# A layered attention and gated-GLU kernel: a new feature layout with the first chunk projected from raw weights, residual additions that are due on VectorE, and divided attention operations

## The chip, the cores and the metric

The kernel runs on one core of a Trainium2 chip. A core has a matrix engine (TensorE, PE in the profile, PEld for its weight loads), a vector engine (VectorE, DVE), an activation engine (ScalarE, ACT), a general engine (GpSimd, POOL) and a sequencer that issues the transfers here (SyncE, SP). Each engine runs its own queue in order, and semaphores order the engines among each other. Matmuls write to PSUM, eight banks of 128 partitions by 2 KB; everything else lies in SBUF. The metric is device microseconds of one launch, the median of several executions.

## The reference

Input and output are 2048 tokens of 576 features in bf16. Four layers run one after the other, two of kind A and two of kind B in turn, each with a residual: `x = x + A(norm(x))`, `x = x + B(norm(x))`, and the same pair again with the same weights.

- norm is a layer norm without parameters (mean, variance, eps 1e-5).
- A is local attention: `qkv = x @ wqkv` gives 32 heads of 18 features. Query s looks at 8 keys, at s, s-2, ..., s-14; keys before token 0 are masked. Softmax over the 8, the weighted sum of the values, then `@ wo`.
- B is a gated bilinear block: `h = (x @ w_gate) * (x @ w_up)`, 4608 wide, then `h @ w_down`.

## The kernel before

The tokens are worked off in chunks: `seq` lists 18 of them as (layer pair, first tile, number of 128-token tiles). The first four chunks of the first layer pair have one tile, the other 14 have two. The tokens go in two groups of eight tiles, and within a group first layer pair 0 and then layer pair 1. For every chunk j the program states the operations of `attention(j, ...)` and then of `glu(j, ...)`.

The order of the instructions is not that of the program. Each operation is given to a planner (`Plan.op`) with its engine, an estimated cost in ns, the keys that it reads and writes, a priority and a rank. `Plan.run` (lines 84 to 166) simulates the engines with these estimates and emits operations one by one; within an engine that order is then fixed. It takes the operation that can start first. Where that one has a rank above 0, an operation of a lower rank on the same engine is taken instead if it becomes ready soon enough (SLACK, GUARD, IDLE and LOOK set how soon). Chunk 0's attention has rank 0, chunk j's attention rank j, all GLU work 60; operations marked `due=True` have rank -1. These are the evacuations of the GLU (L901 on ScalarE, L902 on VectorE) and the small copies of `fence` (L471). Where TensorE would wait early on, `fill` (L1067) emits matmuls on zeros.

Attention of a chunk: `head` norms the tokens (bn_stats L414, aggregate L415, rstd by Ln and Exp on ScalarE L429 and L430, the scaled mean L433, the apply L439) and transposes them, for the first five chunks on TensorE (L452, L454) with a copy by ScalarE (L457), later by a DMA. `project` makes q, k and v (L527), which ScalarE, and for chunk 0 VectorE too, bring to SBUF. Scores: VectorE multiplies q with shifted k for two of the eight positions at a time (L676), adds feature blocks (L680 to L685; not for chunk 0), and TensorE adds over the features with the selector Esel (L691). Softmax: the mask for the first tokens (L710), max, subtract, Exp, sum, reciprocal, multiply (L711 to L722). The weights are spread to the features' partitions: for the first five chunks by matmuls with Bsel (L732), later over DRAM (`a_dram`, one write and four reads). VectorE multiplies them with shifted v (L762) and adds (L776; for chunk 0 matmuls with the identity do that, L766 and L767). Then come the output projection (L816 for one tile, L795 for two) and the residual additions on VectorE (L786), two for each tile, and the second `head` for the GLU.

The projection wants the features by (feature, head) and not by (head, feature). So wqkv is loaded in its own order into the scratch area `scr` (L323, q and k first, v after) and 25 copies (L355, 12 on VectorE and 13 on ScalarE) bring it into `wqkv` in the new order. Chunk 0's projection waits for these copies.

The GLU block works in units of 512 columns: gate and up (L866 and L877 for one tile, L890 for two) into a pair of banks, ScalarE copies the gate (L901), VectorE multiplies (L902), TensorE does the down projection (L918 and L919, or L958 and L959), and VectorE adds its result (L929, L938). Output projection and q, k, v use the same pairs of banks ("unit"). The GLU weights come in six slices of columns, the wd tiles in a ring of seven.

```python
    for j, (l, t0, nst) in enumerate(seq):
...
        pool["k"] = "pa" if j else "boot"
        pl.rank = min(j, 50)
        attention(j, l, t0, nst)
        pl.rank = 60
...
        glu(j, t0, nst, l == n_al - 1)
```

Of the kernel before, what the change touches and what calls it, by code (L numbers as in the profile page):

```python
# [16 lines left out]
class Op:  # L17
    __slots__ = ("eng", "cost", "fn", "deps", "order", "succ", "n", "prio", "idx", "hold", "free",
                 "lat", "margin", "ready", "end", "nbytes", "use", "pair", "need", "rank", "late", "half")
# [3 lines left out]
HOLD = 2  # L23
VP = ["ACT"] * 5
VT = ["ACT"] * 5
SLACK = {"DVE": 500, "ACT": 300, "PE": 0, "POOL": 0, "SP": 0}
IDLE = (2000, 300)
GUARD = {"DVE": 300, "ACT": 300, "PE": 600, "POOL": 0, "SP": 0}
TURN = (148, 98)
LOOK = {"DVE": 1, "ACT": 1, "PE": 1, "POOL": 0, "SP": -9}  # L30


class Plan:
# [13 lines left out]
    def op(self, eng, cost, fn, r=(), w=(), prio=1, after=None, hold=None, free=None, margin=0, nbytes=0, use=None,  # L47
           pair=None, need=None, due=False, late=0, half=False):
        o = Op()
        o.rank, o.late, o.half = -1 if due else self.rank, late, half  # L50
# [3 lines left out]
        d = set()  # L54
# [28 lines left out]

    def run(self, slots):
        clock = {e: 0.0 for e in self.LAT}
# [5 lines left out]
        while cand:  # L91
            best = None
            urgent = {}
            for o in cand:
                t = 0.0
                for p in o.deps:
                    e = p.ready if p.eng != o.eng else p.end
                    if e > t:
                        t = e
                t += o.margin  # L100
                if o.hold is not None:
# [10 lines left out]
                t = max(t, clock[o.eng])  # L112
                key = (t, o.prio, o.idx)
# [5 lines left out]
            if o.rank > 0:  # L119
# [34 lines left out]
            if o.free is not None:  # L154
# [3 lines left out]
                if u["left"] == 0:  # L158
                    free[o.free].append((u["last"], u["slot"]))
            o.fn()  # L160
            done += 1
            for s in o.succ:
                s.n -= 1
                if s.n == 0:
# [5 lines left out]
def kernel(  # L170
# [33 lines left out]
    NXS, NWD, NH, NXB, NB = 4, 7, 6, 3, 3  # L204

# [8 lines left out]
    a_dram = [dram.tile([P, 2 * CH], BF16, name=f"a_dram{i}") for i in range(2)]  # L214
# [12 lines left out]
    Bsel = sb("Bsel", [P, 4, 4, 32])  # L227
# [31 lines left out]
    wrawa = scr[:, 0:KT * 2 * D].rearrange("p (k n) -> p k n", k=KT)  # L259
    wrawb = scr[:, 7168:7168 + KT * D].rearrange("p (k n) -> p k n", k=KT)  # L260
# [41 lines left out]
    def load_x(t0, nst, tmp=False):  # L302
# [3 lines left out]
           nbytes=P * nst * D * 2, prio=0 if t0 < 1 else 1.5 if t0 < 2 else 2.5)  # L306
# [11 lines left out]
    def load_w(c):  # L318
        wr, c0, c1 = ((wrawa, 0, 2 * D), (wrawb, 2 * D, 3 * D))[c == "b"]
        for k in range(KT):  # L320
            for r_, rows in ((0, P),) if k < KF else ((0, TL), (TL, TL)):
                def fn(k=k, r_=r_, rows=rows):
                    i = nc.sync.dma_start(wr[r_:r_ + rows, k, :], A_wqkv[k * P:k * P + rows, c0:c1])  # L323
# [777 lines left out]
```

## Time and profile before

| What | Value |
|---|---|
| median of 3 executions | 1062.14 us (1060.86 to 1063.78) |
| profiled execution, its own time | 1063.46 us |
| its span, first to last instruction | 1061.7 us |
| mean granted TensorE clock | 0.996 |
| busy: TensorE, VectorE, ScalarE | 98%, 74%, 39% |
| first GLU matmul | 33.88 us |
| VectorE busy, 60 to 150 us | 77.8 of 90 us |
| VectorE busy, 200 to 600 us | 341.6 of 400 us |
| VectorE busy, 900 to 1000 us | 47.1 of 100 us |

A row of the timeline has start and length in us, engine, line, operation, output <- input, shape and count, and in brackets the engine's idle time before it and what ended that. A row of the waits has who waited for whom, us in total, times and the longest. PEclk is the clock that TensorE was granted, as a share of the full one. A window's row has its bounds, its length, the busy time of the engines asked for, the clock, the DMA engines' mean busy share and their GB/s.

### The profile page before, as it was taken

Reading aid. Unit: us, or ns where it says so; the run is one execution under the profiler, and the core shown is the slowest. Engines: PE = TensorE matmul, PEld = TensorE weight load, DVE = VectorE, ACT = ScalarE, POOL = GpSimd, SP = SyncE. Lnnn points to the kernel's source line nnn. Section 1 sums busy time; section 2 is a strip of 40 time slices with the busy share of each in tenths; the row PEclk is TensorE's granted clock in tenths of the full one; section 3 lists DMA queues with packets and bytes.
Section 4 is the critical chain, followed back from the end, with each engine's and each line's share of the span. In section 5 each row is a group of like instructions: output and inputs, shape, how many; then the busy total and the mean of one; then the engine's idle time right before and its main releaser. Section 6 shows DMA issues by size and latency. Waiting matters only on the chain.

```text
span 1061.7 us, 39938 instructions
## 1 busy us (share of the span) xinstructions
PE 1044.4 (98%) x17864; PEld 839.5 (79%) x17864; DVE 781.6 (74%) x1421; ACT 411.8 (39%) x1090; POOL 8.9 (1%) x33
## 2 busy tenths in 40 slices
PE   7999999999999999999999999999999999999998
PEld 4888878798888878878878887777877778877775
DVE  7688979786969896989798874666788748833332
ACT  6752254342334534423444324324334252233231
POOL 3000000000000000000000000000000000000000
PEclk9999999999999999999999999999999999999999
DMA  9956563623253444345444443243362333443332
GB/s 263 323 184 197 179 178 102 170 69 121 81 147 86 128 103 109 82 126 138 117 93 106 110 143 94 83 147 87 75 173 82 94 94 115 126 127 102 114 102 68
DMA packets 146827, 133.67 MB, mean 126 GB/s; under 512 B 42272, under 2 KB 146016, under 8 KB 146656
## 3 DMA queue, kind: packets, MB, share of 16 engines
q1 hardware_dynamic: 146656, 131.13, 44.1%
q8 instruction: 139, 2.28, 0.9%
q14 instruction: 32, 0.26, 0.1%
HBM read 118.51 MB, written 4.06 MB: 115 GB/s over the span
## 4 chain that ended last, share of the span: by engine, by line
PE 77%; DVE 14%; DMA 5%; ACT 1%; SPq 1%; issue 1%; DVEq 0%; ACTq 0%
PE pu L890 15%; PE pg L890 13%; PE pu L958 5%; PE acct L890 4%; PE pa L958 4%; PE pa L890 4%; PE pg L527 4%; PE pu L527 3%; PE pg L958 3%; PE acct L958 3%; PE pu L866 3%; PE pg L866 3%; PE pg L918 3%; DVE scr L762 2%; DVE oT L776 2%; DVE h L902 2%
## 5 line engine op out<-in xcount | busy, mean ns | idle before, releaser
L890 PE MATMUL pg<-xnT_B,wg 64*128 64x256 bf16 x3072 | 394.8, 270 | 3.2 <-DVE xf L786 3.2
L890 PE MATMUL pu<-xnT_B,wu 64*128 64x256 bf16 x3072 | 394.3, 270 | 1.6 <-DVE xf L938 1.2
L890 PEld LDWEIGHTS <-wg 64*128 64x128 bf16 x4032 | 367.3, 94 | 28.6 <-issue 3.4
L890 PEld LDWEIGHTS <-wu 64*128 64x128 bf16 x4032 | 366.3, 94 | 24.6 <-issue 3.6
L902 DVE TENSOR_TENSOR h<-pu,g_sb 128x512 bf16<-128x512 f32 x228 | 153.7, 686 | 59.4 <-ACT g_sb L901 56.0
L958 PEld LDWEIGHTS <-h 64*128 64x128 bf16 (+1 forms) x1992 | 120.7, 94 | 96.9 <-DVE h L902 1.6
L901 ACT CAST g_sb<-pg 128x512 bf16<-128x512 f32 x228 | 132.2, 586 | 115.8 <-PE pg L890 80.6
L471 ACT COPY tok<-pu 1x1 f32<-1x1 f32 x270 | 39.7, 147 | 308.8 <-PE pu L890 214.5
L959 PE MATMUL pg<-wd,h 64*128 64x64 bf16 (+1 forms) x828 | 157.4, 190 | 1.4 <-DVE xf L786 1.4
L959 PE MATMUL pu<-wd,h 64*128 64x64 bf16 (+1 forms) x828 | 157.4, 190 | 0.3 <-DVE xf L786 0.2
L958 PE MATMUL pg<-wd,h 64*128 64x512 bf16 x600 | 154.9, 377 | 0.3 <-DVE h L902 0.3
L958 PE MATMUL pu<-wd,h 64*128 64x512 bf16 x600 | 154.9, 377 | 0.0
L890 PE MATMUL acct<-xnT_B,wg 64*128 64x256 bf16 x960 | 130.7, 269 | 0.0
L890 PE MATMUL pa<-xnT_B,wu 64*128 64x256 bf16 x960 | 130.7, 270 | 0.0
L959 PEld LDWEIGHTS <-h 64*128 64x128 bf16 (+1 forms) x1992 | 119.2, 95 | 2.1 <-issue 1.7
L527 PEld LDWEIGHTS <-wqkv 64*128 64x128 bf16 (+1 forms) x2044 | 103.9, 94 | 15.5 <-issue 3.8
L676 DVE TENSOR_TENSOR scr<-qT,kv 128x2560 bf16<-128x2560 bf16 (+1 forms) x68 | 89.9, 1326 | 29.9 <-ACT kv L611 29.7
L958 PE MATMUL acct<-wd,h 64*128 64x512 bf16 (+1 forms) x396 | 103.6, 382 | 0.4 <-DVE h L902 0.4
L958 PE MATMUL pa<-wd,h 64*128 64x512 bf16 (+1 forms) x396 | 104.0, 382 | 0.0
L890 PE MATMUL pu<-xnT_B,wgu_t 64*128 64x256 bf16 x384 | 103.5, 270 | 0.0
L890 PE MATMUL pg<-xnT_B,wgu_t 64*128 64x256 bf16 x384 | 103.5, 269 | 0.0
L527 PE MATMUL pg<-xnT_A,wqkv 64*128 64x256 bf16 (+2 forms) x853 | 96.3, 261 | 0.1
(155 smaller groups left out, 1645.9 us busy)
## 6 DMA issues: line engine op xcount, KB each, us to landing
wd<-in_B_w_down_dram SPq DMA_DIRECT2D x324, 288.0 KB, 4.5
scr<-a_dram SPq DMA_DIRECT2D x52, 128.0 KB, 2.8
wg<-in_B_w_gate_dram SPq DMA_DIRECT2D x6, 768.0 KB, 9.4
wu<-in_B_w_up_dram SPq DMA_DIRECT2D x6, 768.0 KB, 10.9
out_dram<-xf SPq DMA_DIRECT2D x16, 144.0 KB, 3.2
xb<-in_A_x_dram SPq DMA_DIRECT2D x6, 288.0 KB, 2.9
a_dram<-scr SPq DMA_DIRECT2D x13, 128.0 KB, 2.8
scr<-in_A_wqkv_dram SPq DMA_DIRECT2D x4, 288.0 KB, 4.3
```

The source lines that it names most:

```text
L471: box["at"] = nc.scalar.copy(tok[0:1, :], src())
L527: return nc.tensor.matmul(bank(p_, u)[0:m, e * n:(e + 1) * n], lhsT=wqkv[r_, k, w0:w0 + m], rhs=xnT_A[r_, k, c0:c0 + n], start=start, stop ...
L676: nc.vector.tensor_tensor(late["prod"][p_ % 2][:, :, :, 0:n], q2, k2, op=ALU.mult)
L762: nc.vector.tensor_tensor(js(dst), js(vT[:, :, o0:o0 + n]), abw, op=ALU.mult)
L776: op("DVE", 70 + 2.63 * n, lambda i_=i_: nc.vector.tensor_tensor(oT[:, :, 0:n], oT[:, :, 0:n], late["prod"][i_ % 2][:, 0, :, 0:n], op=ALU. ...
L866: nc.tensor.matmul(pt[:, e * n:(e + 1) * n], lhsT=w_[:, k, ft * P:(ft + 1) * P], rhs=xT[:, k, 0:n], start=(first and k == 0 and e == 0), s ...
L890: return nc.tensor.matmul(ps[:, e * n:(e + 1) * n], lhsT=w_, rhs=xT[rows, k, 0:n], start=(first and e == 0 and k == 0), stop=(not first an ...
L901: op("ACT", 490, lambda: nc.scalar.copy(g_sb[gs][:, 0:ul], pg[use["slot"]][:, 0:ul]), r=[f"wg_{j}_{u}"], w=[f"g{gs}"], prio=0, due=True)
L902: op("DVE", 605, lambda: nc.vector.tensor_tensor(hb[hs][:, 0:ul], pu[use["slot"]][:, 0:ul], g_sb[gs][:, 0:ul], op=ALU.mult), r=[f"wu_{j}_{ ...
L918: nc.tensor.matmul((pg, pu)[i][use["slot"]][:], lhsT=lhs, rhs=wt[:, e % 2, 0:512], start=first, stop=fin)
L958: return [lambda: nc.tensor.matmul((pg, pu)[i][use["slot"]][:], lhsT=lhs, rhs=wt[rows, e % 2, 0:512], start=first, stop=fin, skip_group_ch ...
L959: lambda: nc.tensor.matmul((pg, pu)[i][tl["slot"]][:, 0:TL], lhsT=lhs, rhs=wt[rows, e % 2, 512:D], start=first, stop=fin, skip_group_check ...
```

## The change

Seven things are changed together.

1. Feature layout: the 576 features of q, k and v are numbered as 64 half heads of 9 features instead of 32 heads of 18. The selectors, the rows of wo and the layout of `a_dram` follow. wo is loaded by three DMAs instead of six, and the spread over DRAM reads with two DMAs instead of four, with the four j blocks of a head lying together.
2. Raw weights: wqkv is loaded into the columns of `wg` and `wu` that GLU slices 4 and 5 fill later. Chunk 0 projects from there (`raw64`): each matmul of 128 columns becomes two of 64, and its weights are read with a step of 9 elements. It waits for the loads alone. The copies into `wqkv` now serve chunks 1 and later; they have rank 1, and the planner chooses VectorE or ScalarE for each. Slices 4 and 5 wait for the projection and the copies. The second x tile is loaded ahead of the weights; v's weights wait for the second instead of the third load of q and k.
3. Planner: `ahead` first simulates the operations up to the end of chunk 0's attention without the others and notes the start of each (`res`). In the real run, operations of rank 1 and above keep out of these times.
4. Residual additions of two-tile chunks get `due=True`.
5. Divided operations: the score product of two-tile chunks into one per position; the first softmax step into max and subtract; sum and reciprocal; statistics of the early norms by halves; for chunk 0's second norm the apply and the copy after the transpose, shared by ScalarE and VectorE.
6. Chunk 0's weighted sum uses four product buffers instead of two, and its second accumulator bank is taken only when the spread weights are there (`r=abk`).
7. Several constants of the planner's estimates change (GUARD, margins, expected landing times).

The core of the diff:

```diff
-GUARD = {"DVE": 300, "ACT": 300, "PE": 600, "POOL": 0, "SP": 0}
+GUARD = {"DVE": 50, "ACT": 50, "PE": 100, "POOL": 0, "SP": 0}
+TOL = {"DVE": 100, "ACT": 100, "PE": 100, "POOL": 1e9, "SP": 1e9}
...
+    def ahead(self, slots, last):
+        every, emit = self.ops, self.fill
+        ops = [o for o in every if o.idx < last and o.rank < 1]
...
+        for o in ops:
+            o.fn = lambda: None
+        self.ops, self.fill = ops, None
+        self.run(slots)
...
+        for o in ops:
+            if o.rank == 0 and o.cost and o.eng != "SP":
+                o.res = o.end - o.cost
...
+                if o.alts:
+                    o.eng = min(o.alts, key=lambda e: (clock[e] + o.alts[e], e))
+                    o.cost, o.lat = o.alts[o.eng], self.LAT[o.eng]
...
+                if o.rank >= 1 and o.cost:
+                    for b0, c0, _, _ in book[o.eng]:
+                        if t + o.cost > b0 + shift + TOL[o.eng] and t < b0 + shift + c0:
+                            t = b0 + shift + c0
...
-    wrawa = scr[:, 0:KT * 2 * D].rearrange("p (k n) -> p k n", k=KT)
-    wrawb = scr[:, 7168:7168 + KT * D].rearrange("p (k n) -> p k n", k=KT)
+    R0 = 4 * F // FS
+
+    def raw(t3, k):
+        if k == KF:
+            return wu[:, t3, R0 + D:R0 + 2 * D]
+        return wg[:, k, R0 + t3 * D:R0 + (t3 + 1) * D] if t3 < 2 else wu[:, k, R0:R0 + D]
+
+    def raw64(r_, k, c):
+        t3, d = (c // 512, c % 512 // 64) if c < 1536 else ((c - 1536) // 64, 8)
+        return raw(t3, k)[r_].rearrange("p (x d) -> p d x", d=9)[:, d]
...
+                box["o"] = op("ACT", costs["ACT"], fn, r=rk, w=[key], prio=2.5, alts=costs)
...
-                   w=[f"{nm}{s}"], nbytes=P * KF * fw * 2, prio=4 + s)
+                   w=[f"{nm}{s}"] + rawk * (s >= 4), nbytes=P * KF * fw * 2, prio=4 + s)
...
-           r=mk + rk, w=nk, prio=prio)
+           r=mk + rk, w=nk, prio=0 if on_pe else prio)
...
+            if halves:
+                op("ACT", 490, lambda i=i: nc.scalar.activation(xn[ia + i][:, 0:320], src(i)[:, 0:320], ACT.Identity,
...
+                op("DVE", 330, lambda i=i: nc.vector.tensor_scalar(xn[ia + i][:, 320:D], src(i)[:, 320:D], rstd[:, ia + i:ia + i + 1],
...
+                if j < NRAW:
+                    for hf in range(w0 == 1600, 2):
+                        nc.tensor.matmul(bank(p_, u)[TL * hf:TL * hf + TL, e * n:(e + 1) * n], lhsT=raw64(r_, k, w0 + TL * hf), rhs=xnT_A[r_, k, c0:c0 + n],
+                                         start=start, stop=stop, skip_group_check=True)
+                    return
...
-            op("DVE", 70 + 5.2 * n, l1, r=qk, w=[pk], prio=prio)
+            if nst == 2:
+                for e in range(2):
+                    op("DVE", 70 + 2.6 * n, lambda p_=p_, e=e: nc.vector.tensor_tensor(
+                        late["prod"][p_ % 2][:, e, :, 0:n], qT[:, :, 0:n], kT[:, :, HALO - DIL * (2 * p_ + 1 - e):HALO - DIL * (2 * p_ + 1 - e) + n], op=ALU.mult),
+                       r=qk, w=pk, prio=prio)
+            else:
+                op("DVE", 70 + 5.2 * n, l1, r=qk, w=pk, prio=prio)
...
-            for g in range(4):
-                op("SP", 600, lambda g=g: nc.sync.dma_start(late["ab"][32 * g:32 * g + 32, :, 0:W * sq],
-                                                            dr[:, 0:W * sq].rearrange("(j h) n -> h j n", j=4)),
-                   r=[f"adr{j % 2}", "ab"], w=[f"ab{g}"], prio=0, nbytes=P * W * sq * 2, late=1200)
+            for g in range(2):
+                op("SP", 600, lambda g=g: nc.sync.dma_start(late["ab"][TL * g:TL * g + TL].rearrange("p j n -> p (j n)"),
+                                                            dr[:].unsqueeze(1).to_broadcast([H, 2, 8 * CH])),
+                   r=[f"adr{j % 2}", "ab"], w=[f"ab{g}", f"ab{g + 2}"], prio=0, nbytes=2 * P * W * sq * 2, late=1200)
...
-                    ob0 = op("PE", 0, lambda: None, w=[bo[1].key], prio=0, hold=bo[1].pool, use=bo[1].use)
+                    ob0 = op("PE", 0, lambda: None, r=abk, w=[bo[1].key], prio=0, hold=bo[1].pool, use=bo[1].use)
...
-                       prio=prio - 1, free="unit", use=us[i])
+                       prio=0, free="unit", use=us[i], due=True)
...
     load_x(0, 1)
     setup_a()
+    load_x(1, 1)
     load_w("a")
-    load_x(1, 1)
     load_w("b")
...
+        pl.ahead(room, boot)
+        pl.run(room)
```

More of the change, by code (lines that the diff above doesn't have):

```diff
@@ new lines, in perm, with fn @@
+                    dst = wqkv[:, k, t3 * 512:(t3 + 1) * 512].rearrange("p (d x) -> p d x", d=8)
+                    parts, costs = [(dst, src)], {"DVE": 560, "ACT": 1020}
+                else:
+                    tt = (0, 1) if t3 == 3 else (2,)
+                    parts = [(wqkv[:, k, 1536 + 64 * t:1600 + 64 * t], raw(t, k).rearrange("p (x d) -> p d x", d=9)[:, 8, :]) for t in tt]
+                    costs = {"DVE": 110 * len(tt), "ACT": 200 * len(tt)}
+                box = {}
+                def fn():
+                    for d_, s_ in parts:
+                        {"DVE": nc.vector.tensor_copy, "ACT": nc.scalar.copy}[box["o"].eng](d_, s_)
```

199 lines of the change are left out of this document (124 added, 75 removed).

## The prediction

> **What bounds the kernel now.** I read the page's first two parts, then the stretches by window, then the first 34 us instruction by instruction, then TensorE's own waits.
>
> ```profile
> PE 1044.4 (98%) x17864; PEld 839.5 (79%) x17864; DVE 781.6 (74%) x1421; ACT 411.8 (39%) x1090; POOL 8.9 (1%) x33
> PE   7999999999999999999999999999999999999998
> PEclk9999999999999999999999999999999999999999
> ```
>
> TensorE is the bound: 98% busy at nearly the full clock. What the change doesn't take from TensorE's work it can only win where TensorE waits or runs fillers: the start, and a few gaps. The start is everything up to the first gate matmul of the first GLU block at 33.88 us; it follows one chain through VectorE, ScalarE and TensorE:
>
> ```profile
> 4.85 5.55 DVE L355 COPY wqkv<-scr 128x512 bf16<-128x512 bf16 x12
> 11.28 0.99 DVE L609 CAST kv<-pu 128x512 bf16<-128x512 f32 x2
> 12.38 3.03 DVE L676 TENSOR_TENSOR scr<-qT,kv 128x1280 bf16<-128x1280 bf16 x4
> 15.32 0.81 DVE L414 BATCH_NORM_STATS2 st<-xb 128x6 f32<-128x288 bf16 x2
> 16.41 0.27 DVE L710 TENSOR_TENSOR pu<-pu,cap 32x112 f32<-32x112 f32 x1
> 20.90 0.38 PE L732 MATMUL pu<-scr,Bsel 128*128 128x256 bf16 x2 [0.24 <-ACT scr L611]
> 22.15 3.94 DVE L762 TENSOR_TENSOR scr<-kv,scr 128x640 bf16<-128x640 bf16 x8
> 30.91 0.11 DVE L433 SCALAR_TENSOR_TENSOR nmr<-mv,rstd 128x1 f32<-128x1 f32 x1
> 31.05 0.87 ACT L439 ACTIVATE xn<-xf,nmr,rstd 128x576 bf16<-128x576 f32 x1 [0.42 <-DVE nmr L433]
> 32.59 0.69 ACT L457 COPY xnT_B<-pg 128x640 bf16<-128x640 bf16 x1 [0.67 <-PE pg L454]
> 33.88 1.07 PE L866 MATMUL pg<-xnT_B,wg 128*128 128x128 bf16 x16
> ```
>
> To be seen: the permutation copies (L355) stand before the first evacuation, the next chunk's statistics (L414) stand between the scores and the softmax, and the second spread (L732) waits for ScalarE to empty the first one's bank. After 34 us TensorE's idle time is short; its list of waits:
>
> ```profile
> PE pg L890 <- DVE xf L786: 3.2, 3, 1.7
> PE pg L959 <- DVE xf L786: 1.4, 1, 1.4
> PE pu L890 <- DVE xf L938: 1.2, 3, 0.5
> ```
>
> L786 is the residual addition that frees the two PSUM units of the output projection. The longest such wait, with VectorE's rows and two windows of 2 us (length, TensorE busy, granted clock, DMA share, GB/s):
>
> ```profile
> 380.82 1.49 DVE L676 TENSOR_TENSOR scr<-qT,kv 128x2560 bf16<-128x2560 bf16 x1
> 382.22 0.45 DVE L786 TENSOR_TENSOR xf<-pg,xf 128x288 f32<-128x288 f32 x1
> 384.00:386.00 2.00, 2.00 (x25) 0.60 0.04 8
> 386.00:388.00 2.00, 2.00 (x22) 0.55 0.83 203
> ```
>
> The projection's last matmuls start at 381.0, but a score product 1.49 long stands ahead of the additions; TensorE starts again only at 382.72, and then runs 4 us at a clock of 0.575 in the mean, 4 x 0.425 = 1.7 us lost. From 600 us to 1040 TensorE is busy throughout.
>
> **The change, part by part.** The profiled execution took 1063.46 us: a span of 1061.7 and 1.76 around it. The median shown is 1062.14, 1.32 lower. Differences below are made on the profiled execution and taken off the median.
>
> *Raw projection of chunk 0.* The copies leave the path. The weights' landings remain: the last of the q,k part landed at 9.08. The second x tile (147 KB) is moved ahead of them in SP's queue; at the 1.2 us per 295 KB between the q,k landings that is +0.6, so 9.7. Ten tail matmuls pair up in about 0.6, so the evacuations start near 10.5 instead of 11.21 to 11.28: -0.75. Each 128-column matmul becomes two of 64 columns. For two column groups the nearest row is the four-group one: twenty Esel matmuls of 64 columns started within 0.135 us, 7 ns each, a quarter of their 27 ns, so groups run side by side and a pair should cost what one matmul did (55 ns between starts at 7.48). Bounds: nothing, or, if strided weight reads go like the strided L355 copy (609 ns for 512 elements, 1.2 ns each) and the halves don't overlap, 36 x 0.15 = 5.4 for the full rows and 19 x 0.08 = 1.5 for the tails, 7.48 + 6.9 = 14.4, that is 3.9 later than 10.5. I take nothing: the Esel row is a weight load of the same engine.
>
> A rule of the Trainium skill speaks against this part: the page "SBUF — State Buffer", section "Door 1: The DMA port swizzle", has reads in lines of 16 bytes, with a penalty where each access falls in a new one; the raw weights are read at 18 bytes. No row here shows TensorE reading weights so; by the row above the start gains 3.1, by the rule it would gain less or nothing.
>
> *Copies moved, not removed.* 25 copies (12 on VectorE, 13 on ScalarE) go into gaps of both engines. VectorE ran nothing else from 4.93 to 10.31, and ScalarE little else from 11.85 to 17.70: cost 0. If that cover is gone, chunk 1's attention is late; its normalized input was ready at 74.22 for a GLU start at 81.26, so 7.0 us are free. GLU weight slices 4 and 5 now wait in SP's queue for the copies (done by 19.32 before) and stand behind nothing that is needed early: they were issued from 39.74 and landed by 58.52; unchanged. The weight loads behind them in the queue (wd) shift with them only if a copy ran after 39.7. SP issues three wo loads fewer and two a_dram loads fewer per late attention (0.45 to 0.6 each); at a DMA share of 1.0 from 12 to 60 us that gains nothing early, and later VectorE's 36.9 us of waiting for a_dram may shrink, which is idle time beside TensorE: 0.
>
> *Statistics in halves, reserved times.* VectorE's cap operation (L710) came at 16.41 behind L414 and L415; the last Esel matmul started at 15.6 and took 0.2, so 0.55 more goes: -1.3 in all at this point.
>
> *Second spread's bank.* The idle accumulator bank is no longer taken ahead. The first spread was evacuated 20.26 to 20.84, the second 21.37 to 22.06; with both banks free and both engines at once the second ends near 21.1 (by the old clock): -1.0.
>
> *First chunk's second norm.* nmr goes ahead of chunk 2's statistics: rstd ended at 30.63, nmr came at 30.91: -0.25. The apply (0.87) is split 320/256 columns over both engines: about -0.3; the copy (0.69) likewise, -0.2. Sum of the start: 0.75 + 0.55 + 1.0 + 0.25 + 0.3 + 0.2 = 3.05, and the GLU would start near 30.8. It doesn't stop on weights: slice 0 had landed by 24.36, slice 1 by 29.98 and is first needed 2 us into the block.
> Bounds: nothing gained (3.9 lost at the loads, less 3.05), to 4.5 (the GLU's own 0.6 behind other matmuls at 33.28 goes too).
>
> *Residual additions due, score product in two.* One L676 of 1.48 becomes two: L676 on half the size took 0.82, starting 0.74 apart when back to back. An addition now waits for at most one such piece. The four stalls, with the restart's 0.26 to 0.34: 0.96 at 221, 2.12 at 382.7, 1.88 at 537.7, 1.37 at 587.2, together 6.3. At 221, 382.7 and 587.2 the additions can start only about 0.65 to 0.7 earlier, since the first half is already running; at 537.7 they stood behind three more operations, and the whole 1.6 goes: 3.6. The clock's 1.7 follows the longest gap (1.86); the 1.54 gap at 536 had none. Cut to 1.2 it may go: half, 0.85. Sum 4.45. Bounds: 0, or all 8.0. Price: 56 products get 0.08 longer, 4.5 us of VectorE over 500 us at some 85%; TensorE doesn't see it. If VectorE waits idle for an addition, the h products (L902) behind it wait too, and the down projection for these. What is late next: the L938 settles (1.2) and h (0.7), which I leave standing.
>
> On the clock, the Trainium skill ("TensorE: Matmul & The Clock Gate", section "Why this matters for your kernels") has it drop after gaps of some 3 us; the row here has 0.55 to 0.60 after 1.86. By the row the loss can go with the stall, by the rule it wouldn't.
>
> *The rest* (softmax and statistics divided, patterns of the selectors, layout of wo and of a_dram): the same elements by the same engines, less than 0.1 us per attention on VectorE: 0.
>
> Sum: 3.05 + 4.45 = 7.5 from 1063.46 gives 1055.96 for an execution like the profiled one, and 1062.14 - 7.5 = 1054.6 at the median.
>
> **The rivals.** (1) Strided raw weights are slow: the start ends 3.9 - 3.05 = 0.85 later than before, the stalls still go: 1062.14 + 0.85 - 4.45 = 1058.5. For it: no row shows such a load. Against it: loads up to 0.07 per column half would still hide behind the landings.
> (2) The stalls move: TensorE waits for the same time on L938 or h; only the start is won: 1059.1. For it: VectorE is 85% busy to 600 us. Against: the stalls sit at additions alone, and h waits come to 0.7.
> (3) The start is won but chunk 1 is late by more than its 7.0 us, so TensorE waits for it: only the stalls are won: 1057.7.
> (4) Slower: VectorE's order is fixed, and it now holds the additions ahead of GLU products. At each of the 14 two-tile chunks, where VectorE reaches its four additions before TensorE has finished the output projection, it stands still and the h products behind it are late. From 0.22 us of TensorE per chunk (3.05/14) beyond the stalls it eats the start's gain, from 0.45 it makes the kernel slower by the bound; at the 0.8 of one score piece it gives 1062.14 - 3.05 + 11.2 = 1070.3. For it: full VectorE. Against: between 600 and 1000 us VectorE is at 47 to 75% and can wait.
> (5) Nothing changes: TensorE's other work absorbs both: 1062.1.
>
> **How the numbers follow.** Forecast 0.54, (1) 0.12, (2) 0.12, (3) 0.08, (4) 0.12, (5) 0.02. The bound of 0.3%, about what this kernel's measurement can tell from no change, is 3.2 us: 1058.9 and 1065.3. Faster: 0.52 of the forecast, 0.10 of (1), 0.05 of (2), 0.07 of (3): 0.74. Slower: (4) and 0.01 of (1): 0.13. Same: 0.13. Range: from the start's 4.5 with all 8.0 of the stalls and some of the other waits (1048) to just below nothing gained (1062); outside it lie (4) and a few in a hundred below.
>
> **What would show it.** Right: no L355 copy ahead of the first evacuation, which starts by 10.6; spreads back to back; first gate matmul near 30.8; L786 gone from TensorE's waits; the clock at 1.00 near 385. Wrong: projection matmuls of chunk 0 more than 60 ns per pair apart, chunk 1's GLU waiting, VectorE idle in front of L786's successor with TensorE waiting for h, or new gaps after 600 us.

## The result: slower, by TensorE's waits for VectorE

| | before | after |
|---|---|---|
| median | 1062.03 us | 1077.61 us (1075.51 to 1078.01) |
| profiled execution, its own time | 1063.46 us | 1077.90 us |
| its span, mean clock | 1061.7 us, 0.996 | 1076.1 us, 0.997 |
| first GLU matmul | 33.88 us | 34.03 us |
| TensorE's stalls after 36 us | 9.7 us | 24.0 us |

The ratio is 1.0138, with a 95% interval of 1.012 to 1.0156. The forecast was 1054.6 us, so the kernel is 15.6 us slower than before where 7.5 us were to be won.

A stall is counted here as a stretch above 0.25 us between the starts of two matmuls beyond the time of the first one's columns. The stalls grew by 14.3 us and the start by 0.15; together 14.45, and the two profiled executions lie 14.44 apart. So the loss is in TensorE's stalls, to within some 2 us: the 1.7 us that the slow clock near 385 us cost before is gone too, so waits too short to count must have grown by about as much. The start won nothing. The page after, its engines and its slices:

```profile
PE 1046.3 (97%) x17900; PEld 844.4 (78%) x17918; DVE 786.3 (73%) x1481; ACT 410.9 (38%) x1093; POOL 10.7 (1%) x33
PE   8999999999999999999999999999999999999998
PEclk8999999999999999999999999999999999999999
```

TensorE is still the bound; its busy time grew by 1.9 us only. The first digit of the clock fell from 9 to 8: the start before had one stretch at 0.50 (16 to 18 us), the start after has two (8 to 11 us, and 18 to 20 us at 0.51). From here on a settle is the addition of a down projection's result to the features (L938 before, L1034 after), and an h product is gate times up (L902 before, L998 after); both run on VectorE, and TensorE waits for the banks that they free and for the data that they make. Rows of TensorE's list of waits after, and below them VectorE's wait for the spread, after and then before (who waited for whom, us, times, longest):

```profile
PE pg L1054 <- DVE h L998: 4.5, 7, 1.0
PE pg L986 <- DVE xf L1034: 3.3, 5, 1.3
PE pu L986 <- DVE xf L1034: 3.0, 6, 0.7
...
DVE oT L858 <- DMA scr<-a_dram: 59.0, 13, 7.5
DVE oT L762 <- DMA scr<-a_dram: 36.9, 11, 6.1
```

The residual addition, at the top before, is gone from the list. In its place stand the h products and the settles, which in the list of before had 0.7 and 1.5 us; counted as stalls, 11.2 us are at h and 9.9 at settles, where it was 1.0 and 2.4. And VectorE's waiting for the spread has grown from 36.9 us to 59.0. How the two belong together shows in one place, rows of the timeline around 634 us:

```profile
625.10 0.59 SPq L836 DMA_DIRECT2D a_dram<-scr  x1
625.93 0.69 DVE L998 TENSOR_TENSOR h<-pu,g_sb 128x512 bf16<-128x512 f32 x1 [0.18 <-ACT g_sb L997]
628.47 1.76 SPq L839 DMA_DIRECT2D scr<-a_dram  x2
634.13 0.83 DVE L858 TENSOR_TENSOR oT<-kv,scr 128x1280 bf16<-128x1280 bf16 x1 [7.51 <-DMA scr<-a_dram]
634.87 0.82 DVE L858 TENSOR_TENSOR scr<-kv,scr 128x1280 bf16<-128x1280 bf16 x1
635.61 0.68 DVE L1034 TENSOR_TENSOR xf<-pg,xf 128x512 f32<-128x512 f32 x1
636.35 0.27 PE L986 MATMUL pg<-xnT_B,wg 64*128 64x256 bf16 x1 [1.27 <-DVE xf L1034]
```

The softmax weights are written to DRAM at 625.10 and read back from 628.47; the next thing in VectorE's fixed order is the first weighted product, and VectorE stands idle in front of it for 7.51 us. The settle at 635.61 frees a pair of banks. Its data were ready earlier (the down projection's last matmuls for it start at 632.05), but it comes behind two products, and TensorE stops for 1.27 us. This is at 634 us, where the kernel before had no stall at all: 700 to 800 us now has 96.56 us of TensorE in 100.

### The profile page after: what moved, and what is told of

It reads as the page before. It is cut to its first block, busy times and chain, and to the rows that moved or that the text cites. A ratio compares the mean times of both kernels' runs of the same rounds, so it can differ in the third digit from the quotient of the medians.

```text
span 1076.1 us, 40042 instructions
## 1 busy us (share of the span) xinstructions
PE 1046.3 (97%) x17900; PEld 844.4 (78%) x17918; DVE 786.3 (73%) x1481; ACT 410.9 (38%) x1093; POOL 10.7 (1%) x33
## 3 DMA queue, kind: packets, MB, share of 16 engines
q8 instruction: 140, 2.29, 0.9%
## 4 chain that ended last, share of the span: by engine, by line
PE 62%; DVE 24%; DMA 9%; ACT 2%; issue 1%; SPq 1%; POOL 0%; DVEq 0%; ACTq 0%; POOLq 0%
PE pu L986 10%; PE pg L986 10%; PE pu L1054 8%; DMA scr<-a_dram 5%; DVE h L998 5%; DVE scr L858 4%; DVE oT L872 4%; PE pg L1054 4%; DMA a_dram<-scr 4%; PE acct L986 3%; PE pa L986 3%; PE pu L962 3%; PE pg L962 3%; PE pg L611 3%; PE pu L611 3%; PE pg L1014 3%
## 5 line engine op out<-in xcount | busy, mean ns | idle before, releaser
L1054 PE MATMUL pg<-wd,h 64*128 64x512 bf16 (+1 forms) x948 | 246.0, 377 | 5.2 <-DVE h L998 4.5
L1054 PE MATMUL pu<-wd,h 64*128 64x512 bf16 (+1 forms) x947 | 246.5, 377 | 0.0
L998 DVE TENSOR_TENSOR h<-pu,g_sb 128x512 bf16<-128x512 f32 x224 | 151.3, 684 | 72.2 <-ACT g_sb L997 68.7
L986 PE MATMUL acct<-xnT_B,wg 64*128 64x256 bf16 x1024 | 139.4, 269 | 0.0
L986 PE MATMUL pa<-xnT_B,wu 64*128 64x256 bf16 x1024 | 139.3, 269 | 0.0
L611 PEld LDWEIGHTS <-wqkv 64*128 64x128 bf16 (+1 forms) x1974 | 100.5, 94 | 15.4 <-issue 5.8
L1055 PE MATMUL pu<-wd,h 64*128 64x64 bf16 (+1 forms) x588 | 111.2, 189 | 1.0 <-DVE h L998 1.0
L1055 PE MATMUL pg<-wd,h 64*128 64x64 bf16 (+1 forms) x588 | 111.2, 189 | 0.0
L781 DVE TENSOR_TENSOR scr<-qT,kv 128x1280 bf16<-128x1280 bf16 x104 | 81.9, 815 | 25.8 <-ACT kv L695 25.8
L872 DVE TENSOR_TENSOR oT<-oT,scr 128x1280 bf16<-128x1280 bf16 (+1 forms) x119 | 90.9, 764 | 2.9
L611 PE MATMUL pg<-xnT_A,wqkv 64*128 64x256 bf16 (+1 forms) x786 | 88.8, 262 | 1.4 <-DVE xf L1034 1.0
L611 PE MATMUL pu<-xnT_A,wqkv 64*128 64x256 bf16 (+2 forms) x756 | 87.1, 263 | 1.6 <-DVE h L998 1.1
```

Of the source, the lines that this page charges most:

```text
L611: return nc.tensor.matmul(bank(p_, u)[0:m, e * n:(e + 1) * n], lhsT=wqkv[r_, k, w0:w0 + m], rhs=xnT_A[r_, k, c0:c0 + n], start=start, stop ...
L781: op("DVE", 70 + 2.6 * n, lambda p_=p_, e=e: nc.vector.tensor_tensor(late["prod"][p_ % 2][:, e, :, 0:n], qT[:, :, 0:n], kT[:, :, HALO - DI ...
L872: op("DVE", 70 + 2.63 * n, lambda i_=i_: nc.vector.tensor_tensor(oT[:, :, 0:n], oT[:, :, 0:n], late["prod"][i_ % 2][:, 0, :, 0:n], op=ALU. ...
L986: return nc.tensor.matmul(ps[:, e * n:(e + 1) * n], lhsT=w_, rhs=xT[rows, k, 0:n], start=(first and e == 0 and k == 0), stop=(not first an ...
L998: op("DVE", 605, lambda: nc.vector.tensor_tensor(hb[hs][:, 0:ul], pu[use["slot"]][:, 0:ul], g_sb[gs][:, 0:ul], op=ALU.mult), r=[f"wu_{j}_{ ...
L1054: return [lambda: nc.tensor.matmul((pg, pu)[i][use["slot"]][:], lhsT=lhs, rhs=wt[rows, e % 2, 0:512], start=first, stop=fin, skip_group_ch ...
```

## The start: what was to be won there

Rows of the timeline of the kernel after, for the rows that the prediction showed of before:

```profile
12.30 0.60 ACT L729 ACTIVATE qT<-pg 128x512 bf16<-128x512 f32 x1 [1.36 <-PE pu L608]
14.32 0.27 ACT L722 ACTIVATE qT<-pu 64x128 bf16<-64x128 f32 x1 [1.42 <-PE pu L608]
15.02 1.56 DVE L760 TENSOR_TENSOR scr<-qT,kv 128x1280 bf16<-128x1280 bf16 x2
18.16 0.63 DVE L416 COPY wqkv<-wu 128x512 bf16<-128x512 bf16 x1
18.82 0.27 DVE L800 TENSOR_TENSOR pu<-pu,cap 32x112 f32<-32x112 f32 x1
22.98 0.69 DVE L693 CAST scr<-pu 128x512 bf16<-128x512 f32 x1 [0.49 <-PE pu L826]
23.77 3.31 DVE L858 TENSOR_TENSOR scr<-kv,scr 128x640 bf16<-128x640 bf16 x8
31.65 0.16 DVE L497 SCALAR_TENSOR_TENSOR nmr<-mv,rstd 128x1 f32<-128x1 f32 x1 [0.20 <-ACT rstd L494]
33.18 0.29 DVE L533 COPY xnT_B<-pg 128x256 bf16<-128x256 bf16 x1 [0.30 <-PE pg L526]
33.50 0.48 ACT L531 COPY xnT_B<-pg 128x384 bf16<-128x384 bf16 x1 [0.53 <-DVE xnT_B L533]
```

The first evacuation comes at 12.30 (before 11.21, forecast 10.5), the first score product at 15.02 (before 12.38). The last piece of q shares a bank with v's, and its evacuation (14.32) waited behind v's matmuls. From there the steps give back what was lost: first product to nmr took 16.63 us after and 18.53 before, and nmr to the GLU 2.38 and 2.97.

## The experiments

Two theories were tested on the late stalls. **A**: the planner's fixed order expects the spread's weights on chip earlier than they come; VectorE then stands at the first weighted product with settles and h products queued behind it. **W**: the round trip over DRAM has grown because of the new layout's write. Against them stood the additions that are due, the number of reads, and the start.

A word on the measure. The planner's constants give a time from the write's issue to the last read's landing. Before, it is 0.6 us for the write's issue, four times 0.6 for the reads', 0.41 for the bytes of the last one, 2.0 for every landing and 1.2 for `late`: 6.61. After, it is 1.2 for the issue of the write and of the first read, 2 x 0.82 for the bytes of the two long reads, and the same 3.2: 6.04. In neither does the read wait for the write's landing, since an operation on the same engine follows the end of the other's issue (`p.ready if p.eng != o.eng else p.end`); on the chip it is issued 1.72 us after it at the soonest (e5). Measured from the write's issue to the first weighted product, the mean over the 13 late chunks is 7.39 us before and 8.59 after. The plan was short by 0.78 us before, and by 2.55 after; this difference is called the shortfall. Ratios are to the kernel before on the same chip.

**e1: Four reads instead of two** (the kernel after, each read halved).

```diff
-            for g in range(2):
-                op("SP", 600, ... late["ab"][TL * g:TL * g + TL] ... dr[:] ..., late=1200)
+            for g, b in ((0, 0), (1, 0), (0, 1), (1, 1)):
+                op("SP", 600, ... late["ab"][TL * g:TL * g + TL, 2 * b:2 * b + 2] ... dr[:, 4 * CH * b:4 * CH * b + 4 * CH] ..., late=1200)
```

> The changed kernel with the spread over DRAM read by four DMAs of 128 KB again (two halves of the j blocks for each half of the partitions) in place of two of 256 KB; the planner's figures for one such read are those of the kernel before. Theory A (late spread): the weights land about 1.2 us later after the change (write to first weighted product 8.6 us in the mean over 13 chunks against 7.4), while the plan by its own figures expects them 0.8 us sooner, so VectorE stands at its first weighted product with settles and GLU products queued behind. Then the round trip falls to 7.2 to 7.8 us, most stalls of TensorE behind these waits go (some 12 us, more with what trails), and the time is 1060 to 1066 us. Theory B (the residual additions held ahead of GLU products): no change, 1075 to 1080. Theory C (VectorE has more to do because its products are divided): no change, 1075 to 1080.

1070.23 us, ratio 1.0086 (1.0069 to 1.0103): 7.4 us better than after. The round trip did not fall to 7.2 to 7.8 as expected (8.57), so the two long reads are not why it is longer, and the time missed the 1060 to 1066 that a shorter round trip was to give. What changed is the plan's figure, which four issues bring back to 6.61; stalls went from 24.0 to 15.4. Halving the reads helped through what the plan assumes, and not through the transfer.

**e2: The plan expects the spread 2.0 us later** (the kernel after, one number).

```diff
-                   ... nbytes=2 * P * W * sq * 2, late=1200)
+                   ... nbytes=2 * P * W * sq * 2, late=3200)
```

> The changed kernel with only the planner's expected landing of the two reads put 2.0 us later (late 3200 in place of 1200); the DMAs are the same. Theory A: what costs is not the latency but that VectorE's order was made for an earlier landing; with the right expectation other work is placed ahead of the first weighted product: 1061 to 1068, the round trip stays at 8.3 to 8.9 us. If the later landing alone costs, through attention that is late as a whole: 1075 to 1079. Theories B and C: 1075 to 1080.

1057.50 us, ratio 0.9962 (0.9947 to 0.9977): 20 us better than after, and better than before. The same instructions on the same engines, the same transfers, only another order (and with it, for some, another bank). In VectorE's list of waits the line of the spread goes from 59.0 to:

```profile
DVE oT L858 <- DMA scr<-a_dram: 10.7, 8, 3.5
```

Stalls fell to 6.4. The transfer itself is not faster (8.93 to the product).

**e3: The residual additions not due** (the kernel after, part 4 undone).

```diff
-                       prio=0, free="unit", use=us[i], due=True)
+                       prio=prio - 1, free="unit", use=us[i])
```

> The changed kernel with the residual additions of two-tile chunks not due (rank and priority as before). Theory B: the stalls at settles and h products go, 1062 to 1067. Theory A: they stay, and TensorE's waits for the residual additions come back with 3 to 6 us: 1078 to 1085. Theory C: about the same as A.

1077.84 us, ratio 1.0155 (1.014 to 1.017): no difference from after. Stalls 23.8, of which 3.0 at additions again, 8.0 at settles and 11.3 at h. The additions ahead of GLU work are not what makes the kernel slower.

**e4: Contiguous raw weights** (the kernel after; chunk 0 reads 64 neighbouring columns instead of every ninth, so it projects with the wrong columns of the weights; all else is as it was).

```diff
-        return raw(t3, k)[r_].rearrange("p (x d) -> p d x", d=9)[:, d]
+        return raw(t3, k)[r_][:, 64 * d:64 * d + 64]
```

> The changed kernel whose chunk 0 reads 64 neighbouring columns of the raw weights for each half matmul in place of every ninth; it projects chunk 0 with the wrong columns and so leaves the right selection out, all else is the same. Theory R (the step of 18 bytes slows the weight loads): the loads take some 0.1 us in place of 0.21, pairs of half matmuls follow at 55 to 65 ns in place of 116, the q,k part ends about 2 us sooner, and the first GLU matmul comes at 31.5 to 33 us in place of 34.0: 1074.5 to 1076.5. Rival (two column halves don't overlap, whatever the step): pairs stay at 105 to 120 ns, no change.

1072.77 us, ratio 1.0105 (1.009 to 1.012): 4.8 us better than after. The weight loads of chunk 0, in the groups by line and shape (durations min/median/max in ns), after and then here:

```profile
L608 PEld LDWEIGHTS <-wg x72: 190/211/216, 6.9 to 11.3; 128*64 128x64 bf16 x72
L608 PEld LDWEIGHTS <-wu x63: 186/211/215, 11.6 to 15.4; 128*64 128x64 bf16 x36, 64*64 64x64 bf16 x27
```

```profile
L608 PEld LDWEIGHTS <-wg x72: 106/173/178, 6.9 to 10.7; 128*64 128x64 bf16 x72
L608 PEld LDWEIGHTS <-wu x63: 103/107/110, 11.0 to 13.4; 128*64 128x64 bf16 x36, 64*64 64x64 bf16 x27
```

A load with a step of 18 bytes takes 211 ns and one of the same size without a step 107 (the 173 is the stretch at half clock). In a steady run, pairs of half matmuls start 116 ns apart in the mean with the step, at a clock of 0.50 (8.0 to 11.1 us of after) as at 1.00 (12.5 to 14.1 us; e3 above, whose order at the start is that of after, has the first stretch at 1.00 too, and also 116). Without the step they start 56 ns apart at full clock (from 11.5 us here), which is what one matmul of 128 columns took before, and 107 ns apart at 0.50 (7.6 to 10.8 us). So at full clock halving the matmuls costs nothing and the step costs a factor of two; at half clock the step costs 9 ns of 116. The first score product came at 13.18 and the GLU at 31.85, 2.2 us sooner than after; 3.2 us of late stalls went too, with the order of the instructions unchanged, and the time came out below the 1074.5 to 1076.5 expected.

**e5: The write described as four blocks** (the kernel before; the DRAM buffer gets an unused row after each 32, so the write's outermost dimension is 4 and not 128; the bytes, the four reads and the order on VectorE, ScalarE and SyncE stay as they were).

```diff
-    a_dram = [dram.tile([P, 2 * CH], ...
+    a_dram = [dram.tile([4, 33 * 2 * CH], ...
-            dr = a_dram[j % 2]
+            dr = a_dram[j % 2].rearrange("j (h n) -> j h n", h=33)[:, 0:32]
```

> The kernel before; only the DRAM tile of the spread gets one unused row behind each block of 32, so that the one write of 128 KB is described as 4 x 32 rows with a jump and no longer as 128 rows in a line. Every engine's order and the plan stay the same. Theory W (the changed kernel's round trip is longer because its write, which has the four j blocks outermost as well, is spread over fewer DMA engines): the write lands 0.8 to 1.2 us later (3.4 to 3.6 us in the mean against 2.6), the round trip grows from 7.4 to 8.2 to 8.6, the plan is then short by 1.8 us instead of 0.8, and TensorE's stalls at settles and GLU products grow from 3.4 to some 8 to 13 us: 1066 to 1072. Rival (the reads are what is slower): no change of the landing, 1061 to 1063.

1072.15 us, ratio 1.0112 (1.0094 to 1.013): 10 us lost by the description of a 128 KB write. The rows of SP's queue for one chunk, the kernel before and then this one:

```profile
609.77 0.34 SPq L742 DMA_DIRECT2D a_dram<-scr  x1
611.72 2.72 SPq L745 DMA_DIRECT2D scr<-a_dram  x4
```

```profile
614.67 0.56 SPq L742 DMA_DIRECT2D a_dram<-scr  x1
618.00 1.77 SPq L745 DMA_DIRECT2D scr<-a_dram  x4
```

The first read is issued when the write has landed: 1.95 us after the write's issue before, 3.33 here. Over the 13 chunks the mean is 2.59 before (shortest 1.72), 3.48 here (shortest 3.32) and 3.59 after (shortest 3.34). W is shown: the new layout's write is about 1.0 us slower, because its outermost dimension is the four j blocks. The reads take the same time as before (4.80 and 4.73 us from the first read's issue to the product).

The transfers in two windows in which the write runs alone, 701.09 to 702.81 us of before and then 625.10 to 628.47 of after (the row DMA has the mean busy share of the 16 DMA engines, in tenths, in 40 slices of the window):

```profile
DMA  0000000000000000000468999999641000000000
```

```profile
DMA  0000000000000021313112322222222222200000
```

Both move the same 0.13 MB. Before, it is 144 packets, 16 of them under 512 B, and up to nine tenths of the engines are busy at once; after, it is 132 packets, 4 of them under 512 B, and two tenths for most of the time, which is about four of 16 engines. The write in four blocks (e5, 705.97 to 709.30 us) has 132 packets and two tenths as well. The Trainium skill ("DMA: Bandwidth & Descriptors", section "Rules for kernel authors") says that an outermost dimension of fewer than 16 confines a transfer to at most that many of the DMA engines; the trace agrees with it for the 4 here.

**e6: The plan expects the spread 2.0 us sooner** (the kernel before, one number).

```diff
-                   ... nbytes=P * W * sq * 2, late=1200)
+                   ... nbytes=P * W * sq * 2, late=-800)
```

> The kernel before with only the planner's expected landing of the spread's reads put 2.0 us sooner (late -800 in place of 1200); nothing else of the change. Theory A (the plan's time for the spread against the real one sets the stalls): the plan counts 4.6 us from write to landing where the chip takes 7.4, about as short as in the changed kernel (6.0 against 8.6), so the stalls at settles and GLU products come here too, 15 to 25 us of them: 1073 to 1085. If the stalls come from other parts of the change: 1060 to 1065.

1077.96 us, ratio 1.0161 (1.014 to 1.0182): the kernel before becomes as slow as after with none of the change in it. Its lists of waits read like those of after:

```profile
PE pg L958 <- DVE h L902: 4.7, 6, 1.0
PE pg L890 <- DVE xf L938: 3.0, 3, 1.4
...
DVE oT L762 <- DMA scr<-a_dram: 45.1, 13, 6.0
```

Stalls 24.3 us, as in after (24.0), 14.1 at h and 8.1 at settles.

**e7: The residual additions due, alone** (the kernel before with part 4).

```diff
-                       prio=prio - 1, free="unit", use=us[i])
+                       prio=0, free="unit", use=us[i], due=True)
```

> The kernel before with only the residual additions of two-tile chunks due. Theory D of the prediction (they are what TensorE waits for, 6.3 us in four stalls): those four shrink, 1057 to 1060. Rival (the stalls move to settles and products, as VectorE's order is fixed): the waits for the additions go, others come, 1060.5 to 1064. Rival B (held additions cost): over 1065.

1059.13 us, ratio 0.9978 (0.9968 to 0.9988). Stalls at additions fell from 6.3 to 2.0, those at h rose from 1.0 to 2.7. TensorE's busy time fell by 3.3 us and the clock around 385 us is 1.00. The part is worth 2 to 3 us by itself.

**e8: Late plan and true prices of the start** (the kernel after with `late=3200`, and chunk 0's projection given to the planner at 118 ns per pair, with v's part held back by 3 us).

```diff
-                        o = op("PE", 57 * len(parts) if k < KF else 190 + 28 * len(parts), fn,
+                        o = op("PE", 118 * len(parts) if k < KF else 190 + 56 * len(parts), fn, margin=3000 * (part == 1 and k == 0),
```

> The changed kernel with the later expected landing of e2 and with chunk 0's projection planned at its measured pace (118 ns for a pair of half matmuls in place of 57) and its v part held back by a margin of 3 us, so that q's and k's last evacuations stand ahead of it. Theory R2 (after the slow loads, what holds the first scores is that the v part's matmuls stand between the q,k part and the evacuation of its last rows, which came at 14.32): the first score product comes at 13.0 to 13.6 instead of 15.0 and the first GLU matmul at 32.3 to 33.3 instead of 34.1: 1055 to 1056.5. Rival (the chain is held elsewhere, by the spread and the norm): the GLU starts at 33.7 to 34.3 and the time stays at 1057 to 1058.

1056.86 us, ratio 0.9962 (0.9948 to 0.9977): not told apart from the late plan alone (1057.50). The first score product came at 15.26, not at 13.0 to 13.6, and the first GLU matmul at 34.87, later and not sooner. ScalarE's first evacuation of q started at 13.80 only, behind a norm's apply (12.62) and a copy (13.40), and from 14 to 22 us the granted clock was 0.57 in the mean, against 0.79 in after. So better prices for chunk 0's projection did not mend the start here; with these two differences beside it, the run does not show what keeps it.

**e9: The late plan in the kernel before** (one number).

```diff
-                   ... nbytes=P * W * sq * 2, late=1200)
+                   ... nbytes=P * W * sq * 2, late=3200)
```

> The kernel before with one number of the planner changed: it expects the four reads of the spread to land 2.0 us later (late 3200 instead of 1200). The plan was 0.8 us short of the measured round trip and would now be 1.2 us long. By theory A (stalls come from a plan that is short): VectorE's 36.9 us of waiting at the first weighted product shrink to under 12; of TensorE's 9.7 us of stalls the 2.4 behind settles and the 1.0 behind h go, the 6.3 at residual additions stay: ratio 0.996 to 0.999. Rival: a plan that is long costs as much as one that is short, since VectorE then takes the weighted sums late and chunks are late: ratio 1.000 or above.

1056.62 us, ratio 0.994 (0.9926 to 0.9955): more than expected. Stalls fell from 9.7 to 4.9, and the clock near 385 us was 1.00. That 6.3 us at additions would stay was wrong: 3.7 were left.

**e10: Late plan and due additions in the kernel before.**

> The kernel before with both small edits: residual additions due, and the spread expected 2.0 us later. If the two take away different stalls (6.3 at the additions, 3.4 behind the weighted product), the gains add: 1061.3 - 2.4 - 2.5 = 1056.5, ratio 0.9955. Rival: what the additions displace waits next, as it did in the kernel after, and the pair is no better than the additions alone: 1059, ratio 0.998.

The diff is those of e7 and e9 together. 1052.89 us (1052.67 to 1053.11), ratio 0.9906 (0.9892 to 0.9921): the best version here, with two small edits and nothing else of the change. The gains add, and more (the additions are worth 3.7 us on top of the late plan), so what the additions displace does not wait next when the plan is right. TensorE is busy for 99% of the span, and its longest wait in total, 1.2 us (L1067), is at the start. Stalls after 36 us are down to 1.7 us.

**e11 and e12: two more values for the kernel after**, `late=2200` and `late=4200` in the same place.

> The kernel after with the spread expected 1.0 us later (late 2200): a plan 1.55 us short where after was 2.55 short and the version with 3200 0.55. By theory A the loss grows with the shortfall: between the two, some 1064 to 1069, ratio 1.003 to 1.008, TensorE's stalls near 13. Rival: the order that a particular number gives is chance, and the time bears no relation to the shortfall: outside 1060 to 1073.

> The kernel after with the spread expected 3.0 us later than it was (late 4200). With 3200 the plan was still 0.9 us short of the measured round trip and 6.4 us of TensorE's stalls were left, 4.7 more than in the kernel before with both small edits (e10, 1.7 us, 1052.9), which is also the difference of the two times. By theory A these go too, with a plan that is no longer short: stalls of 2 to 3, 1053 to 1055, ratio 0.992 to 0.995. Rival: what is left in that version are stalls of VectorE's greater work around the first chunks, or of the start, which the number does not touch: 1056.5 to 1058.5, ratio 0.995 to 0.997.

With 2200: 1067.70 us, ratio 1.0043 (1.0026 to 1.006), stalls 12.7. With 4200: 1053.81 us, ratio 0.9928 (0.9911 to 0.9944), stalls 1.9. Both as theory A has it. The kernel after, all of it, is then as good as the kernel before with its two edits, within 1 us. Its 1053.81 lies close to the forecast of 1054.6, but not by the forecast's sum: the first GLU matmul comes at 34.64 there, so the start wins nothing, and all of the gain is in the stalls.

All values of the one number, with what the plan expected from the write's issue to the last landing, the measured time to the first product, and the stalls. Where the plan is long, VectorE may come later than the weights, so there the measured time is only an upper bound.

| kernel | plan | measured | stalls | median |
|---|---|---|---|---|
| before, 2.0 us sooner | 4.61 | 7.34 | 24.3 | 1077.96 |
| after | 6.04 | 8.59 | 24.0 | 1077.61 |
| after, four reads | 6.61 | 8.57 | 15.4 | 1070.23 |
| after, 2200 | 7.04 | 8.50 | 12.7 | 1067.70 |
| after, 3200 | 8.04 | 8.93 | 6.4 | 1057.50 |
| after, 4200 | 9.04 | 9.34 | 1.9 | 1053.81 |
| before, write in four blocks | 6.61 | 8.22 | 16.6 | 1072.15 |
| before | 6.61 | 7.39 | 9.7 | 1062.03 |
| before, 3200 | 8.61 | 8.42 | 4.9 | 1056.62 |
| before, 3200, additions due | 8.61 | 8.30 | 1.7 | 1052.89 |

In the kernel before and in the kernel after, the longer the plan's figure, the fewer the stalls; a chance effect of one order or another would not run the same way through both. The kernel before was itself 0.78 us short and lost some 6 us by it.

## Why the prediction was wrong

**The step that failed** is *the rest*: "layout of wo and of a_dram): the same elements by the same engines, less than 0.1 us per attention on VectorE: 0", together with the sentence that VectorE's waiting for a_dram "may shrink, which is idle time beside TensorE: 0". The layout of `a_dram` changed how the write is cut up, and with two reads for four the plan also came to expect the weights 0.57 us sooner. Together they moved the plan's shortfall from 0.78 to 2.55 us. And the waiting grew from 36.9 to 59.0 us, and was not beside TensorE: VectorE's order is fixed, so its idle time in front of the first weighted product holds up the settles and h products behind it, and TensorE's stalls at these grew from 3.4 to 21.1 us. The 36.9 us stood in the profile of before, with settles and h products behind them in VectorE's rows; the question "what is queued behind this wait" was put to the additions and not to it. Nor did "the stalls sit at additions alone" hold before the change: 3.4 of the 9.7 us were at settles and h products.

**The raw projection** was taken at no extra cost for the strided weights, from the row of the Esel matmuls. That row shows column groups side by side, and this held at full clock (56 ns for a pair without the step); it showed nothing on the step, and the step doubled the load. The sum had -0.75 at the first score product; it measured +2.64 (15.02 against 12.38). Of this 3.4 us difference the step itself is 1.84 (13.18 with contiguous weights), at the clocks of these two executions. The other 1.55 is there without the step too. Some 1.0 of it lies before the first evacuation (11.46 with contiguous weights, 10.5 in the sum): the q and k matmuls ran without a gap from 7.6 to 10.8 us at half clock. The remaining 0.55 lies between evacuation and product (1.72 us instead of 1.17), where the last piece of q waits for v's matmuls in its bank; the sum had neither. The rule of the Trainium skill that spoke against this part ("SBUF — State Buffer", section "Door 1: The DMA port swizzle", lines of 16 bytes) has the sign right: 211 ns for a load against 107. Rival (1) put the start 0.85 us later than before; it came 0.15 later. It was right about the loads, and says nothing of the 14 us of late stalls.

**The other steps of the start**, each against its own price: from the first score product to the cap operation 3.80 us instead of 4.03, a gain of 0.23 where 0.55 was priced, because a permutation copy (18.16) and an nmr took the place of the statistics; from the cap to the end of the second spread 4.85 instead of 5.65, 0.8 for 1.0; nmr behind rstd without a gap, 0.25 as priced; the apply 0.65 instead of 0.87, 0.22 for 0.3. The divided copy after the transpose gained nothing: ScalarE's half waited 0.53 us for VectorE's, so that the two took 0.80 in place of 0.69. The weighted products took 3.31 instead of 3.94, a gain that had not been foreseen.

**The residual additions** went as priced in kind: gone from TensorE's waits, and the clock near 385 us at 1.00 instead of 0.55 to 0.60. The term was 4.45 us; alone it measured 2 to 3, with the right plan 3.7. The price of the divided score product was 4.5 us of VectorE; VectorE's busy time rose by 4.7 with the whole change, and with the plan right TensorE did not see it.

**The rivals.** The kernel is on the side of rival (4), slower by waits on h in a fixed order, but (4) put the cause at the additions; without them due the time is the same, 1077.84. Rival (2), that the stalls move to L938 or h, describes the list of waits, yet at 14 us more and not the same time. Of the signs that the prediction named as proof against it, two came: "new gaps after 600 us", and projection matmuls of chunk 0 more than 60 ns per pair apart (116). Of the signs for it, L786's successor (L882) is gone from TensorE's waits, the clock near 385 us is 1.00, the two spreads run back to back, and the first evacuation waits for no copy (ScalarE was idle for 1.36 us before it); but it came at 12.30 and not by 10.6, and the first gate matmul at 34.03 and not near 30.8.

What stays open: why the start of the kernel after ran at a clock of 0.50 from 8 to 11 us. It had two filler matmuls before 7.2 us instead of four, but e3, with the same two and the same order on VectorE and ScalarE up to 30 us, ran this stretch at 1.00, and its GLU started no sooner (34.21). With the write in four blocks the median rose by 10 us where the stalls rose by 6.9; the two profiled executions lie 8.0 apart (1071.49 and 1063.46), so about 1 us is not accounted for, and the rest is spread between executions.

## What to carry to other kernels

Where an order is fixed ahead of time, compare each transfer's assumed arrival with the measured one first, and look at what stands behind the instruction that waits for it; 1 us of shortfall on 13 transfers cost some 8 to 10 us here, and a plan about 1 us long cost nothing that was seen. Before a layout of a DRAM buffer is changed, look at the outermost dimension of the write as it will be described, not only at its bytes. A change of many parts can be judged only after the plan's numbers are corrected for it: here all of it with the right number (1053.81) and two one-line edits of the old kernel (1052.89) came out the same.

## What the runs showed of the hardware

- A 64-column weight load with a step of 18 bytes takes 211 ns at a clock of 0.50 as at 1.00; without a step it takes 107 at 1.00 and 173 at 0.50. Pairs of such matmuls start 116 ns apart with the step at either clock; without it 56 ns apart at 1.00 and 107 at 0.50. So with the step a faster clock won nothing here.
- A 128 KB write from SBUF to DRAM, described with 4 as its outermost dimension instead of 128, lets the read behind it be issued 3.48 us after it in the mean instead of 2.59, and never under 3.3 instead of 1.72. Its packets kept about two tenths of the 16 DMA engines busy instead of up to nine.
- Two reads of 256 KB and four of 128 KB had the spread on chip at the same time (8.59 and 8.57 us).
- The clock fell to 0.50 from 384.4 to 387.8 us of before (0.60 and 0.55 in windows of 2 us), after a stall of 1.86 us at 382.7, and with `late=2200` in the kernel after (0.50 from 532 to 534 us) after one of 2.29 at 530.9. With four reads it stayed at 1.00 after one of 2.32 at 532.1. So the length of a stall alone did not decide it. Near 385 us it was at 1.00 once the stall there was gone or shorter (1.26 us at 382.3 in the kernel after).
